# Five early expert tiles regrouped as a pair, a single and a pair

## The chip, the cores and the metric

The kernel runs on one core of one Trainium2 chip. The metric is device microseconds of one execution. The kernel before takes 584.12 us, the median of three runs (583.96 to 584.71). Arithmetic is in float32 wherever a result depends on it.

## The reference

Block-sparse attention is followed by a mixture of eight experts, of which each row takes one:

```
scores = scale * q @ k^T, masked to: near blocks, first and last block, 3 sampled blocks
x = softmax(scores) @ v                          # 4 x 8 heads x 768 x 64 -> 3072 rows of 512
logits = normed(x) @ normed(expert_emb)^T / tau  # 8 experts
e = argmax(logits); gate = softmax(logits)[e]
out[row] = gate * (relu(x[row] @ w1[e]) @ w2[e]) # w1: 512 x 1024, w2: 1024 x 512
```

With the inputs of the reference, expert 0 takes 813 of the 1536 rows of the first two sequences.

## The kernel before

**Attention.** 24 chunks of 128 rows go through steps `s` of a loop that writes out the order of all engines by hand (`attention_fast`). Each step has two places, `planned(0)` and `planned(1)`, where small work is inserted: the routing of finished chunks (`route`), the ranks of rows within their expert (`rank`), and, once the first two sequences are routed, the sixteen stages of `dispatch_early`, one at a time. `after_step` (L1573) says which stage goes to which step. The stages at the first half of step 18 and its second half, and at the first half of step 19, are the ones around the lines L968 to L1082.

**Expert tiles.** Rows are collected by expert into tiles of 128. A first tile set, the `NE` = 5 early tiles, needs only the first two sequences; the late tiles (2 mixed, 7 pairs, 4 singles) need all rows. Units run in the order S S S S S (early), then S P P M P S P M P P S P S. A single (`expert_tile`, L1304) does the first product as 32 matmuls of 128 columns (L1314), a relu, and the second product as 8 matmuls of 512 columns (L1341). A late pair (`pair_tile`, L1418) takes two tiles of one expert as one 2 x 2 block problem and does each product as seven block products in place of eight: sums of weight blocks on VectorE (`weight_sums`, L1361), sums of row blocks on GpSimd (`sum_rows`), and sums of relu blocks on VectorE (`ssum`). Each float32 matmul stands in the trace as two records.

**What moves data.** `fetch_rows` (L1227) gathers rows by indirect DMAs that GpSimd issues: one DMA for each of the first two tiles, four for each later one. `prepare` turns them: TensorE transposes (L1290) for the first two, VectorE transposes (L1295) for the others. Weights come through SyncE, in three buffers. Results go out by an indirect DMA from GpSimd (L1353, L1528).

**The order.** After attention each engine's order is made by a planner from the order of the program text, estimated costs, and explicit edges (`issue_after`: queue what follows behind a given instruction on its engine). The last chunk's logits and routing sit in the second product of the first tile; the last ranks and the first, long part of `dispatch_late` come from the second tile; its last VectorE instruction is `k.lanes_made` (L1008); the slots of late rows follow at the end of the third tile (L1019), the quarter addresses (L1044, L1051) in the fourth, and the first late gathers come right behind them.

Of the kernel before, what the change touches and what calls it, by code (L numbers as in the profile page):

```python
# [20 lines left out]
P = 128  # L21
# [10 lines left out]
G = 128  # L32
EARLY = 2
NE = (EARLY * S - E * (G - 1) + G - 1) // G
MIX = 2
# [3 lines left out]
NU = N // G - NE  # L39
# [21 lines left out]
NL = most_places(N - NE * G)  # L61
# [14 lines left out]
UNITS, ORDER = in_order("SPPMPSPMPPSPS")  # L76
UNIT_OF = {i: u for u, unit in enumerate(UNITS) for i in unit}
# [789 lines left out]
def route(k, b):  # L867
# [30 lines left out]
    picked = nc.vector.tensor_tensor(out=oh, in0=pick, in1=wide(m), op=ALU.is_equal).ins  # L898
    yield
# [57 lines left out]


def tile_experts(k, end, tiles, name):

    nc, p = k.nc, k.dp
    past = p.tile([P, tiles, E], F32, name="past")
    nc.vector.tensor_tensor(out=past, in0=k.tile_no[:, 0:tiles].unsqueeze(2).broadcast_to([P, tiles, E]),
                            in1=end.unsqueeze(1).broadcast_to([P, tiles, E]), op=ALU.is_ge)
    ex = p.tile([P, tiles], F32, name="ex")
    nc.vector.reduce_sum(out=ex, in_=past, axis=AX.X)
    yield
    nc.vector.tensor_scalar(out=ex, in0=ex, scalar1=float(E - 1), scalar2=None, op0=ALU.min)  # L968
    expert = k.const.tile([P, tiles], I32, name=name)
    nc.vector.tensor_copy(out=expert, in_=ex)  # L970
    return expert
# [83 lines left out]
def dispatch_early(k):  # L1055
# [6 lines left out]
    full = p.tile([P, E], F32, name="full")  # L1062
    nc.vector.reduce_sum(out=full, in_=more, axis=AX.X)
    yield
    end = yield from add_up(k, full)
    nc.vector.tensor_scalar(out=end, in0=end, scalar1=float(NE), scalar2=None, op0=ALU.min)
    expert = yield from tile_experts(k, end, NE, "expert_e")
    k.experts = [expert]
    k.taken = k.const.tile([P, E], F32, name="taken")
    base = p.tile([P, E], F32, name="base")  # L1070
    nc.vector.memset(base[:, 0:1], 0.0)
    nc.vector.tensor_scalar(out=base[:, 1:E], in0=end[:, 0:E - 1], scalar1=float(G), scalar2=None, op0=ALU.mult)
    nc.vector.scalar_tensor_tensor(out=k.taken, in0=end, scalar=float(G), in1=base, op0=ALU.mult, op1=ALU.subtract)
    yield
    pos = of_expert(k, base, nt, "pos")
    yield
    late = p.tile([P, nt], F32, name="late")
    taken = of_expert(k, k.taken, nt, "taken_t")
# [121 lines left out]
def parts(i):  # L1200

    if i < NE:
        return [i]
# [823 lines left out]
```

## Time and profile before

| | |
|---|---|
| median of three runs | 584.12 us |
| the profiled execution | 586.81 us |
| its span | 584.9 us |
| TensorE busy | 560.5 us |
| VectorE busy | 329.6 us |
| GpSimd busy | 292.5 us |
| ScalarE busy | 189.8 us |
| granted TensorE clock, mean | 0.993 |

The span goes from the first to the last recorded instruction; the profiled execution's own time is 1.9 us longer. A row of the timeline has its start, its length, the engine, the line, the operation with output and inputs, and in brackets the idle time of the engine just before it with what ended that. A merged row (x16) covers records that follow each other. A row of a table by stretches has, for each engine, busy time and records, then the granted clock, the share of the DMA engines and GB/s.

### The profile page before, as it was taken

How to read it: one execution, taken by the hardware profiler on the slowest of the kernel's cores; microseconds unless marked ns; L12 is line 12 of the kernel's file. 1: busy time of each engine (PE TensorE's matmuls, PEld its weight loads, DVE VectorE, ACT ScalarE, POOL GpSimd, SP SyncE). 2: the span in 40 equal slices, each digit the busy share in tenths (PEclk: the TensorE clock that was granted, in tenths of full speed). 3: DMA queues.
4: the chain of work that ended last, by engine and by line, in shares of the span. 5: the costliest groups of instructions: out<-in, count | busy, mean ns of one | idle time of the engine just before them, and what ended most of it. 6: DMA issues, size and time to landing. Idle time of an engine off the chain costs nothing.

```text
span 584.9 us, 19051 instructions
## 1 busy us (share of the span) xinstructions
PE 560.5 (96%) x7790; PEld 469.1 (80%) x7790; DVE 329.6 (56%) x821; ACT 189.8 (32%) x367; POOL 292.5 (50%) x510
## 2 busy tenths in 40 slices
PE   8999999899999999999999999999999999999995
PEld 5889898798899888877776789739978568987994
DVE  4462687368779972339615576366563296636610
ACT  3545666375655554200000123103112113220310
POOL 2729646346766331442255848276355485836010
PEclk9999999899999999999999999999999999999998
DMA  8979789999998861799999986589987589754000
GB/s 213 244 162 220 170 188 188 195 210 208 205 213 194 204 208 41 269 401 369 399 400 400 393 319 205 184 315 351 391 311 258 193 309 394 273 188 173 10 33 24
DMA packets 167528, 140.72 MB, mean 241 GB/s; under 512 B 135227, under 2 KB 137407, under 8 KB 165128
## 3 DMA queue, kind: packets, MB, share of 16 engines
q1 hardware_dynamic: 161272, 126.25, 70.9%
q0 software_dynamic: 5104, 12.90, 6.1%
q8 instruction: 63, 1.03, 0.7%
q10 hardware_dynamic: 1056, 0.26, 0.2%
q14 instruction: 33, 0.27, 0.1%
HBM read 126.76 MB, written 12.90 MB: 239 GB/s over the span
## 4 chain that ended last, share of the span: by engine, by line
PE 48%; issue 12%; DVE 12%; DMA 11%; POOL 8%; SPq 5%; ACT 2%; POOLq 0%; DVEq 0%; ACTq 0%
PE hp L1314 7%; PE av L701 7%; PE hp L1440 6%; PE yp L1341 5%; POOL xg L1227 5%; DMA out_dram<-y,slot_l 5%; SPq L531 4%; PE yp L1489 4%; PE dps L645 3%; DMA vg<-in_v_dram 3%; DMA xg<-x_dram,quarter 3%; PE xg_ps L1489 2%; PE ac L620 2%; PE bps L676 1%; PE ac L623 1%
## 5 line engine op out<-in xcount | busy, mean ns | idle before, releaser
L1227 POOL DMA_INDIRECT xg<-x_dram,quarter x92 | 100.5, 1092 | 30.4 <-issue 24.4
L1314 PEld LDWEIGHTS hp<-xgt,w 128*128 128x128 f32 x576 | 65.6, 192 | 2.5 <-issue 1.2
L1314 PE MATMUL hp<-xgt,w 128*128 128x128 f32 x576 | 66.4, 276 | 0.8 <-DVE own L1298 0.8
L1341 PE MATMUL yp<-w,h 128*128 128x512 f32 x128 | 57.5, 596 | 1.3 <-issue 1.2
L600 POOL COPY kg<-kt 128x128 f32 x176 | 43.2, 296 | 28.8 <-ACT kt L560 21.0
L543 POOL COPY vg<-vt 32x1040 f32<-32x1040 f32 (+1 forms) x45 | 42.8, 951 | 18.5 <-issue 8.1
L1528 POOL DMA_INDIRECT out_dram<-y,slot_l x14 | 14.2, 1011 | 67.1 <-DVE y L1496 58.6
L645 PEld LDWEIGHTS dps<-qt,kg 128*64 128x64 f32 x1408 | 46.7, 138 | 0.8 <-POOL kg L600 0.6
L645 PE MATMUL dps<-qt,kg 128*64 128x64 f32 x1408 | 46.0, 222 | 0.2 <-POOL kg L600 0.2
L1341 PEld LDWEIGHTS yp<-w,h 128*128 128x128 f32 x128 | 23.3, 190 | 27.7 <-issue 26.6
L620 PE MATMUL ac<-qt,kt 128*64 128x128 f32 x352 | 43.0, 274 | 1.2 <-DVE half L1659 0.5
L623 PE MATMUL ac<-qt,kt 128*64 128x256 f32 (+1 forms) x192 | 42.5, 364 | 0.1
L582 DVE COPY qt<-yp 64x512 f32<-64x512 f32 x48 | 32.9, 685 | 12.1 <-PE yp L577 11.7
L620 PEld LDWEIGHTS ac<-qt,kt 128*64 128x64 f32 x352 | 37.8, 137 | 2.1 <-ACT lg L822 0.9
L650 ACT ACTIVATE pd<-dps,bias 128x256 f32<-128x256 f32 x88 | 34.7, 474 | 10.5 <-PE dps L645 10.4
L587 DVE TENSOR_REDUCE kg<-kt 128x128 f32 (+2 forms) x136 | 33.6, 317 | 3.0 <-ACT kt L560 1.2
L701 PE MATMUL av<-vg,pd 128*32 128x65 f32 x1408 | 29.5, 222 | 5.9 <-DMA vg<-in_v_dram 4.9
L701 PEld LDWEIGHTS av<-vg,pd 128*32 128x32 f32 x1408 | 23.0, 109 | 12.1 <-DMA vg<-in_v_dram 7.0
L771 ACT ACTIVATE pac<-x 128x512 f32<-128x512 f32 x24 | 15.1, 631 | 43.8 <-DVE x L766 42.4
L1440 PEld LDWEIGHTS hp<-xgt,w 128*128 128x128 f32 x224 | 26.5, 192 | 3.2 <-issue 3.1
L701 PEld LDWEIGHTS av<-st,pac 128*64 128x64 f32 x704 | 23.3, 141 | 5.8 <-issue 4.7
L1489 PE MATMUL yp<-tsum,ssum 128*128 128x256 f32 x112 | 27.0, 384 | 0.8 <-DVE y L1496 0.5
(320 smaller groups left out, 1120.9 us busy)
## 6 DMA issues: line engine op xcount, KB each, us to landing
w<-in_moe_w_dram SPq DMA_DIRECT2D x38, 2048.0 KB
vg<-in_v_dram SPq DMA_DIRECT2D x132, 128.0 KB
kraw<-in_k_dram SPq DMA_DIRECT2D x32, 192.0 KB
x_dram<-x SPq DMA_DIRECT2D x10, 516.0 KB
qraw<-in_q_dram SPq DMA_DIRECT2D x9, 512.0 KB
w<-in_moe_w_dram SPq DMA_DIRECT2D x8, 512.0 KB
vt<-in_v_dram SPq DMA_DIRECT2D x10, 256.0 KB
vt<-in_v_dram SPq DMA_DIRECT2D x5, 512.0 KB
```

The costliest lines, as they stand in the source:

```text
L543: k.nc.gpsimd.tensor_copy(out=k.vg_ring[s % 2][lanes_of(NRAND, g), g, which(i)], in_=k.vt[m][rows, which(i)])
L600: copy(out=t[:, :, g, lanes_of(s, g)], in_=kt[:, :, bass.ds(shift, BLK)])
L620: nc.tensor.matmul(out[0:D, j, half], lhsT=kt[:, j, at:at + D], rhs=qt[:, j, :, D * half:D * (half + 1)], start=True, stop=True)
L623: nc.tensor.matmul(out[D:P, j, half:2].rearrange("p f h t -> p h f t"), lhsT=kt[:, j, S:S + D], rhs=qt[:, j, :, D * half:P].rearrange("p h ...
L645: nc.tensor.matmul(out[D * r:D * (r + 1), NG * j + g], lhsT=kg[:, j, g, D * r:D * (r + 1)], rhs=qt[:, j, :, cols], start=True, stop=True)
L650: nc.scalar.activation(e[:, :, g].rearrange("p j h t -> p j (h t)"), out.rearrange("p (j g) h t -> p j g (h t)", g=NG)[:, :, g], ACT.Exp, ...
L701: k.nc.tensor.matmul(av[lanes, h // NPAIR, h % NPAIR * P:h % NPAIR * P + D + 1], lhsT=lhsT, rhs=rhs, start=first[0], stop=last, skip_group ...
L1227: k.nc.gpsimd.indirect_dma_start(out=x[:, g], out_offset=None, in_=quarters, in_offset=bass.IndirectOffsetOnAxis(ap=k.quarters[late][:, g, ...
L1314: k.inner = nc.tensor.matmul(hp[:, f, :], lhsT=w1[:, d, (f0 + f) * P:(f0 + f + 1) * P], rhs=xt[:, d, :], start=(d == 0), stop=(d == ND - 1 ...
L1341: k.summed = nc.tensor.matmul(yp, lhsT=h[:, f, :], rhs=w2[:, f, :], start=(f == 0), stop=(f == NF - 1)).ins
L1440: nc.tensor.matmul(ps[:, f], lhsT=left[:, d, f * P:(f + 1) * P], rhs=right[:, d], start=start and f == 0 and d == 0, stop=d == ND // 2 - 1 ...
L1489: nc.tensor.matmul(out, lhsT=left[:, c], rhs=right[:, c], start=start and c == 0, stop=c == half - 1, skip_group_check=True)
```

## The change

The five early tiles are no longer five singles. They are three units: tiles 0 and 1 as a pair, tile 2 as a single, tiles 3 and 4 as a pair (`UNITS`). An early pair does a plain first product, 32 matmuls of 256 columns (`plain_first`), and the second one by seven block products, with weight sums of `w2` and relu sums on VectorE but none for `w1`. It issues the product of the first block first and releases the next transposes behind `z4`.

`dispatch_early` now finds up to two pairs of full tiles and one more full tile per expert; it has four per-row look-ups (`of_expert`) where it had two, and eight small GpSimd instructions. The three weight sets of the early units replace five. Late places `NL` go from 24 to 28, of which 20 run as before.

Rows of tiles 0 and 1 are fetched together in the second half of step 22 into a buffer of the ring of `x` (before: tile 0 in the first half of step 22, tile 1 after attention), and turned in the second half of step 23 and the first half of step 24 (before: tile 1's turn inside the first tile).

The last logits and the last routing move from the second product of the first tile into its first product (after blocks 1, 2 and 4 of 8); the last ranks and the long part of `dispatch_late` follow the first block of its second product. The slots come after block 4 of the second early pair, the quarter addresses and the gathers of the first two late units after its block 6. The transposes of tiles 3 and 4 are no longer queued behind `k.lanes_made`; the weight sums of the second early pair are.

```diff
-    units, order = [[i] for i in range(NE)], []
+    units, order = [[0, 1], [2], [3, 4]], []
+EARLY_AT = [0, 1, ONLY, 2, 3]
...
 def dispatch_early(k):
-    full = p.tile([P, E], F32, name="full")
-    nc.vector.reduce_sum(out=full, in_=more, axis=AX.X)
+    upto = p.tile([P, 2, E], F32, name="pairs_full")
+    nc.vector.reduce_sum(out=upto[:, 1], in_=more, axis=AX.X)
+    nc.vector.reduce_sum(out=upto[:, 0], in_=more[:, :, 1::2], axis=AX.X)
...
+    nc.gpsimd.tensor_tensor(out=used, in0=end, in1=start, op=ALU.subtract)
+    nc.gpsimd.tensor_scalar(out=last, in0=used[:, 0], scalar1=2.0 * G, scalar2=None, op0=ALU.mult)
+    nc.gpsimd.tensor_scalar(out=base, in0=start[:, 0], scalar1=2.0 * G, scalar2=None, op0=ALU.mult)
+    nc.gpsimd.tensor_scalar(out=k.taken, in0=used[:, 1], scalar1=float(G), scalar2=None, op0=ALU.mult)
+    nc.gpsimd.tensor_tensor(out=k.taken, in0=k.taken, in1=last, op=ALU.add)
+    nc.gpsimd.tensor_scalar(out=shift, in0=start[:, 1], scalar1=float(G), scalar2=float(ONLY * G), op0=ALU.mult,
+                            op1=ALU.add)
+    nc.gpsimd.tensor_tensor(out=shift, in0=shift, in1=last, op=ALU.subtract)
+    nc.gpsimd.tensor_tensor(out=shift, in0=shift, in1=base, op=ALU.subtract)
     yield
-    pos = of_expert(k, base, nt, "pos")
+    pos, last_t = of_expert(k, base, nt, "pos"), of_expert(k, last, nt, "last_t")
     yield
-    taken = of_expert(k, k.taken, nt, "taken_t")
+    shift_t, taken = of_expert(k, shift, nt, "shift_t"), of_expert(k, k.taken, nt, "taken_t")
     yield
+    nc.vector.tensor_tensor(out=pos, in0=pos, in1=here, op=ALU.add)
+    nc.vector.tensor_tensor(out=last_t, in0=here, in1=last_t, op=ALU.is_ge)
+    nc.vector.tensor_tensor(out=last_t, in0=last_t, in1=shift_t, op=ALU.mult)
+    nc.vector.tensor_tensor(out=pos, in0=pos, in1=last_t, op=ALU.add)
+    nc.vector.tensor_tensor(out=taken, in0=here, in1=taken, op=ALU.is_ge)
+    nc.vector.scalar_tensor_tensor(out=pos, in0=taken, scalar=2.0 * N, in1=pos, op0=ALU.mult, op1=ALU.add)
...
 def expert_tile(k, i):
-        elif i >= WHOLE:
+        else:
             nc.scalar.activation(h[:, half:NF], hp, ACT.Relu)
-            k.relu = k.lanes_made if i == WHOLE else k.made
-        else:
-            k.relu = nc.vector.tensor_scalar(out=h[:, half:NF], in0=hp, scalar1=0.0, scalar2=None, op0=ALU.max).ins
+            k.relu = k.made
...
+def plain_first(k, i, w1, w2, xt, h, after):
+    nc = k.nc
+    banks = pair_banks(k, i)
+    for f in range(NF):
+        ps = banks[f // 2].rearrange("p (f r) t -> p f r t", r=DUO)
+        for d in range(ND):
+            k.inner = nc.tensor.matmul(ps[:, f % 2], lhsT=w1[:, d, f * P:(f + 1) * P], rhs=xt[:, d], start=d == 0,
+                                       stop=d == ND - 1).ins
+        if f % 2:
+            nc.scalar.activation(h[:, f - 1:f + 1], ps, ACT.Relu)
+        after.get(f, lambda: None)()
+    return second_weights(k, w2, None if k.exact else k.lanes_made if i else k.picked)
...
+    made = subtract(k, z4, a(0, 1), z2), subtract(k, z3, a(0, 0), a(1, 0))
+    k.relu = made[0 if early else 1]
...
+    begin = [(q2, a(0, 1), b21), (q1, a(0, 0), b11)]
+    for n, what in enumerate(begin[::-1] if early else begin):
+        second(*what, n == 0)
...
-        plan += [(s + 9, 0, partial(fetch_rows, n, 0))]
+        plan += [(s + 9, 1, partial(fetch_rows, n, i)) for i in range(WHOLE)]
-        plan += [(s + 10, 1, partial(prepare, n, 0))]
+        plan += [(s + 10 + i, 1 - i, partial(prepare, n, i)) for i in range(WHOLE)]
...
+        fetch_rows(n, WHOLE)
+        expert_tiles(n, {1: halfway, 2: lambda: part_logits(n, NS - 1), 4: last_route, NF: last_rank},
+                     {NF // 2: late_slots, NF - 2: lambda: next(n.late), NF + 3: partial(count_good, n)})
```

## Rows read from the trace of the kernel before

**Rows 1.** The page, first part: busy time, share of the span, instructions.
```profile
PE 560.5 (96%) x7790; PEld 469.1 (80%) x7790; DVE 329.6 (56%) x821; ACT 189.8 (32%) x367; POOL 292.5 (50%) x510
```

**Rows 2.** By stretch: one of attention, the early stage, the late stage.
```profile
180.00:190.00 10.00, 9.63 (x274) 8.79 (x270) 9.48 (x35) 4.92 (x14) 6.73 (x20) 1.00 0.85 210
...
237.10:314.15 77.05, 74.72 (x459) 53.72 (x457) 36.37 (x146) 6.85 (x16) 32.51 (x42) 1.00 1.02 385
...
314.15:577.60 263.45, 261.24 (x1657) 215.78 (x1655) 144.32 (x194) 53.70 (x96) 137.73 (x123) 1.00 0.69 250
```

**Rows 3.** Timeline of TensorE, the five early tiles and the first late units.
```profile
244.53 0.60 PE L1290 MATMUL xg_ps<-ident,xg 128*128 128x128 f32 x4
244.97 4.82 PE L1341 MATMUL yp<-w,h 128*128 128x512 f32 x10
249.63 0.60 PE L781 MATMUL xg_ps<-ident,x 128*128 128x128 f32 x4
...
283.17 0.25 PE L1019 MATMUL slot_ps<-val,lanes 128*128 128x48 bf16 x3 [0.22 <-DVE lanes L1008]
284.16 3.84 PE L1314 MATMUL hp<-xgt,w 128*128 128x128 f32 x32 [0.75 <-DVE own L1298]
...
291.60 7.03 PE L1341 MATMUL yp<-w,h 128*128 128x512 f32 x16
298.46 7.31 PE L1314 MATMUL hp<-xgt,w 128*128 128x128 f32 x64
305.61 3.60 PE L1341 MATMUL yp<-w,h 128*128 128x512 f32 x8
310.39 1.13 PE L1341 MATMUL yp<-w,h 128*128 128x512 f32 x2 [1.19 <-issue]
...
328.17 1.95 PE L1440 MATMUL hp<-xgt,w 128*128 128x128 f32 x16
...
551.41 3.62 PE L1489 MATMUL yp<-w,h 128*128 128x256 f32 x16
554.86 1.89 PE L1489 MATMUL xg_ps<-tsum,h 128*128 128x256 f32 x8
```

**Rows 4.** Timeline of attention, steps 17 to 19: VectorE, and a waiting TensorE.
```profile
178.02 0.98 DVE L943 COPY end<-end 128x4 f32<-128x4 f32 x1
...
187.57 0.25 DVE L978 TENSOR_TENSOR at_e<-oh,base 128x96 f32<-128x96 bf16 x1
...
190.76 0.64 PE L800 MATMUL xg_ps<-xt,en 128*32 128x256 f32 x8 [0.85 <-DVE xt L784]
...
192.84 0.17 DVE L1081 TENSOR_TENSOR pos<-pos,rank 128x12 f32<-128x12 f32 x1
```

**Rows 5.** Timeline of the last step of attention: TensorE and the copy behind it.
```profile
230.25 0.67 PE L701 MATMUL av<-vg,pd 128*32 128x65 f32 x32
230.35 0.69 DVE L784 COPY xt<-xg_ps 128x512 f32<-128x512 f32 x1 [0.89 <-PE xg_ps L781]
```

**Rows 6.** Timeline of GpSimd around the second half of step 22.
```profile
219.00 0.47 POOL L902 TENSOR_TENSOR seen<-seen,oh 128x8 bf16<-128x8 bf16 x2 [5.58 <-DVE oh L898]
```

**Rows 7.** Timeline of VectorE: the late dispatch, weight sums, relu sums.
```profile
263.17 0.16 DVE L1099 TENSOR_TENSOR cnt<-count,taken 128x8 f32<-128x8 f32 x1
...
279.75 3.36 DVE L1008 TENSOR_TENSOR lanes<-lane,low 128x384 bf16<-128x384 f32 x7
...
332.42 1.23 DVE L1361 TENSOR_TENSOR tsum<-w 128x1024 f32<-128x1024 f32 x1
...
341.56 0.69 DVE L1444 TENSOR_TENSOR ssum<-h 128x512 f32<-128x512 f32 x1 [2.92 <-ACT h L1469]
```

**Rows 8.** Timeline of the late gathers: quarter addresses, GpSimd's issues, first row sum.
```profile
288.72 0.27 DVE L1051 TENSOR_SCALAR quarter<-quarter_got,group 128x96 int32<-128x96 f32 x1
...
291.06 0.99 POOL L1227 DMA_INDIRECT xg<-x_dram,quarter  x1 [0.31 <-issue]
...
327.52 0.74 POOL L1412 TENSOR_TENSOR xsum<-xgt 128x256 f32<-128x256 f32 x1
```

More of the change, by code (lines that the diff above doesn't have):

```diff
@@ L1067, in dispatch_early @@
-    expert = yield from tile_experts(k, end, NE, "expert_e")
+    for step in (1, 2, 4):
+        nxt = p.tile([P, 2, E], F32, name=f"early{step}")
+        nc.vector.tensor_copy(out=nxt[:, :, 0:step], in_=upto[:, :, 0:step])
+        nc.vector.tensor_tensor(out=nxt[:, :, step:E], in0=upto[:, :, step:E], in1=upto[:, :, 0:E - step], op=ALU.add)
+        upto = nxt
+        yield
+    edge = p.tile([P, 2, E + 1], F32, name="early_ends")
+    end, start = edge[:, :, 1:], edge[:, :, 0:E]
+    nc.vector.memset(edge[:, :, 0:1], 0.0)
@@ L1327, in expert_tile @@
                 first_sums(k, i)
-        if after and f0 - NF in after:
-            after[f0 - NF]()
     yp = ring(k, "yp", i, 1, k.eps, [P, DM])
@@ L1415, in sum_rows, with add, pair_banks, block @@
     subtract(k, s[3], a(0, 1), s[1], k.nc.gpsimd)
[L1418 to L1426 removed]
+def add(k, out, one, other, engine=None):
+    return (engine or k.nc.vector).tensor_tensor(out=out, in0=one, in1=other, op=ALU.add).ins
+def pair_banks(k, i):
+    return [ring(k, f"hp{f0}", i + j, 2, k.hps, [P, NF // 2, P]) for j in range(2) for f0 in (0, NF // 2)]
+def block(h, r, c):
+    half = NF // 2
+    return h[:, half * c:half * (c + 1), r]
+def second_weights(k, w2, behind):
+    with k.tc.issue_after(behind) if behind is not None else ExitStack():
+        return weight_sums(k, w2, [ring(k, f"tsum{j}", 0, 1, k.wp2, [P, NF // 2, DM // 2]) for j in range(3)])
+def seven_first(k, i, w1, w2, xt, h):
+    nc, half, a = k.nc, NF // 2, partial(block, h)
     (b11, _), (b21, b22) = four_blocks(w1)
@@ L1485, in pair_tile @@
     y0, y1 = (ring(k, "y", i + j, 2, k.wp2, [P, DM]) for j in range(2))
+    made = iter(range(NF, NF + 7))
     def second(out, left, right, start=False):
         for c in range(half):
-            nc.tensor.matmul(out, lhsT=left[:, c], rhs=right[:, c], start=start and c == 0, stop=c == half - 1,
-                             skip_group_check=True)
+            k.inner = nc.tensor.matmul(out, lhsT=left[:, c], rhs=right[:, c], start=start and c == 0,
+                                       stop=c == half - 1, skip_group_check=True).ins
+        after.get(next(made), lambda: None)()
     def scaled(out, ps, gate):
@@ L1847, in expert_tiles @@
         elif second_half:
-            pair_tile(n, i)
+            pair_tile(n, i, hooks.get(i, {}))
         else:
-            expert_tile(n, i, {0: after, 1: second and {NF // 2 - NF: second}, NE - 2: {-NF: first_late},
-                               NE - 1: spread and {NF // 2: partial(count_good, n)}}.get(i))
-        next(between, None)
+            expert_tile(n, i)
 def last_tiles(n):
```

189 lines of the change are left out of this document (89 added, 100 removed).

## The prediction

> **What bounds the kernel now.** I read the page's busy times first: TensorE is busy for 560.5 of 584.9 us [rows 1], so time can only be saved where TensorE has less to do or waits. The table by stretches then splits the span: the five early tiles take 77.05 us with TensorE busy for 74.72, the late units up to the last product 263.45 with 261.24 busy [rows 2]. The granted clock is 1.00 in all of these, the 2.4 GHz level, so no term below is a clock term. Last I read the timeline of TensorE in the early stage, tile by tile, to separate products from insertions and waits [rows 3]. The late units are not touched except in when their rows arrive; I leave their length as it is and price only their start.
>
> The profiled execution took 586.81 us, 1.9 more than its span and 2.7 more than the median of 584.12. All terms below are differences within its span; I subtract them from the median.
>
> **Products (A).** A single's first product starts at 298.46 and its second at 305.61: 7.15 us for 32 matmuls of 128 columns. A second product runs from 291.60 to 298.46: 6.86 us [rows 3]. Two singles are 28.02. In an early pair the second product is seven blocks of four matmuls with 256 columns. In the late pair two such blocks take from 551.41 to 554.86, 3.45 [rows 3], so seven take 12.08, against 13.72. The plain first product is 32 matmuls of 256 columns. The trace has none of that input, but the second product's blocks have the same shape: eight matmuls in 3.45, so 13.80, against 14.30. I take that, as the operation is the same; the upper end is 14.30, if a wider matmul gains nothing. A pair is 25.88, 2.14 less; two pairs 4.28 less (3.28 at the other end). Fewer weight loads are hidden under the matmuls already.
>
> **Waits that go (B).** 77.05 us less five times 14.01 leaves 7.0 us of insertions and waits. Three waits belong to the old form. In the first tile, ten records of the second product should take 4.29 (16 take 6.86) and the next row starts 4.66 later, at 249.63: 0.37, behind a relu that VectorE made late. At the third tile's end TensorE waits 0.22 for the lanes and 0.75 for the fourth tile's rows, which were queued on VectorE behind the lanes: 0.97. In the fifth there is a wait of 1.19 in the middle of the second product [rows 3]. The change gives all early relus to ScalarE, takes the edge to the lanes away from the transposes, and makes the fifth tile half of a pair. I count all three as gone, 2.53. The first two have a named cause that leaves; the third has "issue" as its releaser and may come back, so the low end is 1.34; the high end is 3.7, all of what is left of the 7.0 when the insertions that stay (about 2.9) and 0.44 of transposes are taken out. What the slots of late rows wait for next is VectorE (below).
>
> **Transposes of tile 1 (C).** They take 0.44 in the stage (244.53 to 244.97 [rows 3]) and move into attention's last step, right behind the turn of a chunk into the same PSUM tile. VectorE copies that turn out until 231.04, and TensorE's next work starts at 230.25 [rows 5]. In an order written by hand the new transposes wait there: 0.80 us, and the weighing queued behind them with them. So C is +0.80 net. It is nothing at the low end, should the later wait for ScalarE's exponentials absorb it. The fetch itself is one more GpSimd issue, where GpSimd is idle for 5.58 us before 219.00 [rows 6].
>
> **Early dispatch on VectorE (D).** Two more look-ups of two instructions at 0.25 each are 1.0 us at the second half of step 18, three more small instructions at 0.17 are 0.5 at step 19 [rows 4]; what the earlier stages gain and lose is within 0.4. VectorE is busy for 9.48 of 10 us from 180 to 190 [rows 2], and right after step 18 TensorE already waits 0.85 for a copy by VectorE [rows 4]. There is no cover there: I take the whole 1.5 as lost. It is 0 if VectorE's small idle times take it. Eight small GpSimd instructions come before these look-ups and can make VectorE wait: a copy of four columns took 0.98 on VectorE, others of that size 0.17 [rows 4], while GpSimd copied. Twice that excess, 1.6, is the upper addition, so 3.1 at the high end. The Trainium skill ("SBUF — State Buffer", section "SBUF: two separate sides") says that VectorE and GpSimd hold one port pair by an exclusive lock for a whole instruction, and the 0.98 against 0.17 agrees; by it the eight new instructions would speak for the high end of D, and the sum would be about 1.6 us worse.
>
> **Last routing, ranks, late dispatch on VectorE.** Let zero be the start of the first pair. Its first product lasts 13.80 with 1.45 of insertions (transposes, logits) and its second 12.08 with 0.2 for the ranks, so the single starts at 27.5 and the second pair at 41.5. The last logits come after five of eight blocks, near 10.1, and the last choice of experts near 11.9. VectorE then has: four weight sums at 1.23, 4.9; four relu sums at 0.69, 2.7; the transposes of tile 2, 1.4 with their gate; ranks, 0.7; the late dispatch from 263.17 to 283.11, 19.2 without the result copy inside it, and some 0.6 for NL at 28; three gated results, 1.4 [rows 7]. That ends at 42.9, if the transposes of tiles 3 and 4 (2.8) are elsewhere. The weight sums are done at 16.8 and their first user starts at 15.3 + 3.7 = 19.0: no wait. The lanes are needed after five blocks of the second pair, at 50: no wait. I take 0 for all of this; the danger is in the fourth rival.
>
> **Late rows (E).** Now the quarter addresses are ready at 289.0 [rows 8], 25 us before the first late single at 314.15 [rows 2]. After the change they are ready some 14.6 us into the second pair (seven blocks at 1.73, slots 1.1, addresses and their wait 1.4), which lasts about 27.2: 12.6 us before that single. GpSimd issues a gather every 1.3 [rows 8]. Twelve gathers for the two late units end at 3.7 us after the single's start; the first four land in time. One result, four gathers, one result, four gathers follow, as now eight gathers stand ahead of the first row sum (327.52, against a pair that starts at 328.17 [rows 3, 8]). The sum comes at 17.5 after the single's start; the pair's second block product needs it at 14.0 + 1.8 = 15.8. So TensorE waits 1.7. The ends are 0 (the planner puts the sums ahead of four gathers) and 3.0 (GpSimd's instructions are stretched by 5%, as 23 of them last 30 us).
>
> **Sum.** -4.28 - 2.53 + 0.80 + 1.5 + 1.7 = -2.8. 584.1 - 2.8 = 581.3. Two weight sets of 4 MB fewer are loaded while the DMA engines are at 1.02 of their share [rows 2]; no wait of TensorE in the stage names a weight, so I give nothing for it.
>
> **Rivals.** *1. The additions hide.* D and E are 0: -6.0, 578.1. For it: VectorE is idle by 5% around step 18, and the order of GpSimd is free to put row sums first. Against: the wait of 0.85 names VectorE.
> *2. The saving is half of it.* A is 3.28 and the 1.19 stays: -2.8 + 1.0 + 1.2 = -0.6, 583.5. For it: that wait has no named cause. Against: the same shape is seen at its speed.
> *3. It does not do what it says*: too few full tiles for two pairs, so tiles are computed for nothing and more run at the end, 14 us each. The inputs give expert 0 six full tiles among the early rows, which are three pairs; I leave it at 0.02, near 612.
> *4. The other side: the second pair's rows queue behind the late dispatch.* The planner puts the transposes of tiles 3 and 4 behind the lanes, though no edge asks for it. Then they end at 42.9 + 2.8 = 45.7 and the second pair, due at 41.5, waits 4.2: -2.8 + 4.2 = +1.4, 585.5. For it: the dispatch stands earlier in the text, and the VectorE work between fits only by 1.4 too little. Against: a result copy was let in in the middle of that chain. It decides from where more than about two thirds of the late dispatch stands ahead of both transposes.
>
> **Numbers.** Forecast 0.44 (own range 579.5 to 582.9), rival 1 0.22, rival 2 0.14, rival 3 0.02, rival 4 0.18. A measurement of this kernel can tell 0.2%, 1.17 us, from no change. Forecast and rival 1 are faster, 0.66; rival 2 is the same, and of rival 4 a small part is: 0.16; the rest, 0.18, is slower. The range goes from 577.2 (below rival 1 by the spread of B) to 585.7 (with half of rival 4).
>
> **What would show it.** A: block products of 1.73 and a first product of 13.8 in the early pairs. C and D: the first expert matmul at 239.8 in place of 237.10; much earlier says D is hidden. B: the first late single 69.8 us after that, at 309.6. E: the first late pair at 323.7, and a wait for `xsum` in it. Rival 4 would show as a wait of the second early pair for `own` or `xgt` by VectorE. The prediction is wrong if the early stage, first expert matmul to first late single, is longer than 73 us.

## The result and the profile after

The changed kernel took 592.47 us (median of 4 runs) against 584.41 for the kernel before on the same chip (4 runs): 1.0133, interval 1.0102 to 1.0164. That is 8.1 us slower, where 2.8 less was forecast. The profiled execution took 591.05 (span 589.3), against 586.81.

First the page's busy times, then the table by stretch (the columns of [rows 2]): the whole early stage, and the two blocks of a second product in it that matter below.

```profile
PE 557.4 (95%) x7710; PEld 476.9 (81%) x7710; DVE 347.9 (59%) x846; ACT 194.1 (33%) x377; POOL 304.1 (52%) x520
...
241.27:320.03 78.76, 72.74 (x376) 60.41 (x374) 49.96 (x161) 11.25 (x25) 34.94 (x42) 0.96 0.85 312
...
261.70:265.08 3.38, 3.38 (x10) 2.67 (x9) 2.46 (x9) 0.00 (x0) 2.77 (x3) 0.53 1.02 417
...
313.07:316.57 3.50, 3.50 (x8) 2.85 (x9) 0.24 (x3) 0.00 (x0) 2.58 (x4) 0.51 0.23 59
```

TensorE is busy 3.1 us less than in [rows 1], and the span is 4.4 longer: TensorE has less to do, and more than that was lost in waits. The early stage, forecast at 69.8 us, took 78.76. TensorE's timeline shows where (start, duration, line, operation, and in brackets the idle time before it with what ended it):

```profile
241.27 2.86 PE L1505 MATMUL hp<-xgt,w 128*128 128x256 f32 x12
...
257.03 1.89 PE L1544 MATMUL yp<-w,h 128*128 128x256 f32 x8
261.60 0.19 PE L932 MATMUL rk<-seen,ones_b 128*128 128x56 bf16 x1 [2.68 <-POOL seen L905]
261.70 3.59 PE L1544 MATMUL yp<-w,h 128*128 128x256 f32 x8
...
313.07 3.66 PE L1544 MATMUL yp<-tsum,ssum 128*128 128x256 f32 x8 [3.35 <-DVE y L1552]
316.57 1.89 PE L1544 MATMUL xg_ps<-w,ssum 128*128 128x256 f32 x8
...
320.03 7.31 PE L1336 MATMUL hp<-xgt,w 128*128 128x128 f32 x64
...
334.04 1.95 PE L1469 MATMUL hp<-xgt,w 128*128 128x128 f32 x16
339.06 2.05 PE L1469 MATMUL hp<-xsum,x 128*128 128x128 f32 x16 [1.29 <-POOL xsum L1377]
```

The first expert matmul starts at 241.27 (239.8 was forecast, 237.10 in [rows 2]) and the first late pair at 334.04 (323.7; 328.17 in [rows 3]). The two blocks from 316.57 to 320.03 take 1.73 each, as forecast. But there are two waits that the kernel before does not have in this stage. The matmul that ranks the last routed tokens waits 2.68 for GpSimd's count `seen`; the second pair's fifth block waits 3.35 for VectorE's gated result `y`, whose PSUM bank it needs. Behind each, the next block takes 3.38 and 3.50, twice its time, and the granted clock there is 0.53 and 0.51, the 1.2 GHz level.

What made the two releasers late stands in the queues of their own engines. GpSimd, then two stretches of VectorE:

```profile
254.88 1.14 POOL L909 TENSOR_TENSOR gate<-ex_l 128x2 f32<-128x2 f32 x1
...
256.80 1.81 POOL L1251 DMA_INDIRECT xg<-x_dram,quarter  x1 [0.48 <-issue]
258.64 0.32 POOL L905 TENSOR_TENSOR seen<-seen,oh 128x8 bf16<-128x8 bf16 x1
259.11 1.94 POOL L1251 DMA_INDIRECT xg<-x_dram,quarter  x1 [0.15 <-issue]
261.08 0.47 POOL L905 TENSOR_TENSOR seen<-seen,oh 128x8 bf16<-128x8 bf16 x1
...
254.74 1.23 DVE L1377 TENSOR_TENSOR tsum<-w 128x1024 f32<-128x1024 f32 x1
...
258.94 1.22 DVE L1377 TENSOR_TENSOR tsum<-w,tsum 128x1024 f32<-128x1024 f32 x1
...
311.29 1.08 DVE L1317 STREAM_TRANSPOSE xgt<-xg 128x512 f32<-128x512 f32 x1 [5.66 <-DMA xg<-x_dram,quarter]
...
312.54 0.48 DVE L1552 SCALAR_TENSOR_TENSOR y<-yp,gate,u 128x256 f32<-128x256 f32 x1
```

The two additions to `seen`, 0.3 and 0.5 us long, stand between the gathers of the second pair's rows, near 1.9 us each. The gated result, 0.48 long, stands behind the transposes of the first late single, and these wait 5.66 for that single's gathered rows. In both cases a short instruction that TensorE needs now is queued behind one that serves a later tile.

For `seen` the order alone is not all of it. GpSimd in the kernel before has the same order:

```profile
256.33 0.19 POOL L906 TENSOR_TENSOR gate<-ex_l 128x2 f32<-128x2 f32 x1
...
257.32 1.11 POOL L1227 DMA_INDIRECT xg<-x_dram,quarter  x1 [0.51 <-issue]
258.47 0.21 POOL L902 TENSOR_TENSOR seen<-seen,oh 128x8 bf16<-128x8 bf16 x1
258.84 1.02 POOL L1227 DMA_INDIRECT xg<-x_dram,quarter  x1 [0.16 <-issue]
259.90 0.21 POOL L902 TENSOR_TENSOR seen<-seen,oh 128x8 bf16<-128x8 bf16 x1
```

There the second addition ends at 260.11, and the ranks are asked for at 261.00, 23.9 us after the first expert matmul. In the changed kernel they are asked for 17.5 us after it. And GpSimd takes 6.67 us from the start of `gate` to the end of the second addition, where the kernel before takes 3.78: the instructions that run beside VectorE's sums for the pair's second product, back to back from 254.74 on but for one short pause, got longer. With the lengths of the kernel before, the second addition would end 2.9 us earlier and the wait of 2.68 would be gone (an estimate from these rows). What makes GpSimd slower there was not tested.

### The profile page after: what moved, and what is told of

Read it like the earlier page. It is cut to its first block, busy times and chain, and to the rows that moved or that the text cites. A ratio compares the mean times of both kernels' runs of the same rounds, so it can differ in the third digit from the quotient of the medians.

```text
span 589.3 us, 18923 instructions
## 1 busy us (share of the span) xinstructions
PE 557.4 (95%) x7710; PEld 476.9 (81%) x7710; DVE 347.9 (59%) x846; ACT 194.1 (33%) x377; POOL 304.1 (52%) x520
## 4 chain that ended last, share of the span: by engine, by line
PE 35%; issue 21%; POOL 14%; DMA 14%; DVE 8%; SPq 4%; ACT 2%; POOLq 1%; DVEq 0%; ACTq 0%
POOL xg L1251 8%; PE hp L1469 6%; PE av L703 5%; PE dps L647 4%; DMA xg<-x_dram,quarter 4%; PE yp L1544 4%; DMA out_dram<-y,slot_e 3%; DMA out_dram<-y,slot_l 3%; SPq L533 3%; DMA vg<-in_v_dram 3%; PE hp L1336 2%; PE xg_ps L1544 2%; PE ac L622 2%; PE ac L625 2%; POOL xsum L1377 2%
## 5 line engine op out<-in xcount | busy, mean ns | idle before, releaser
L1251 POOL DMA_INDIRECT xg<-x_dram,quarter x92 | 103.0, 1120 | 33.4 <-issue 25.4
L1544 PE MATMUL yp<-tsum,ssum 128*128 128x256 f32 x144 | 36.0, 395 | 3.6 <-DVE y L1552 3.3
L1336 PEld LDWEIGHTS hp<-xgt,w 128*128 128x128 f32 x320 | 36.5, 192 | 0.3
L1336 PE MATMUL hp<-xgt,w 128*128 128x128 f32 x320 | 36.5, 275 | 0.0
L1544 PEld LDWEIGHTS yp<-tsum,ssum 128*128 128x128 f32 x144 | 28.2, 198 | 8.5 <-DVE y L1552 4.5
L1552 DVE SCALAR_TENSOR_TENSOR y<-xg_ps,gate,u 128x256 f32<-128x256 f32 x16 | 7.7, 482 | 45.5 <-PE xg_ps L1544 33.3
L1544 PE MATMUL yp<-w,h 128*128 128x256 f32 x144 | 34.4, 393 | 0.0
L1544 PE MATMUL xg_ps<-w,ssum 128*128 128x256 f32 x144 | 34.0, 379 | 0.0
L1549 ACT ACTIVATE u<-yp,gate 128x256 f32<-128x256 f32 x24 | 11.4, 473 | 62.1 <-PE yp L1544 62.1
```

The lines of the kernel that those rows point to most:

```text
L1251: k.nc.gpsimd.indirect_dma_start(out=x[:, g], out_offset=None, in_=quarters, in_offset=bass.IndirectOffsetOnAxis(ap=k.quarters[late][:, g, ...
L1336: k.inner = nc.tensor.matmul(hp[:, f, :], lhsT=w1[:, d, (f0 + f) * P:(f0 + f + 1) * P], rhs=xt[:, d, :], start=(d == 0), stop=(d == ND - 1 ...
L1544: k.inner = nc.tensor.matmul(out, lhsT=left[:, c], rhs=right[:, c], start=start and c == 0, stop=c == half - 1, skip_group_check=True).ins
```

## The experiments

Two theories stood at the start. The main one: those two orders cost the time, each with its half-clock block. The rival: the losses lie elsewhere, in attention (terms C and D) or in stretches in which TensorE waits for nothing that the trace names; then taking the waits away gains little. Kernels that ran together on one chip share the runs of the kernel before on it, and ratios are to these. "Stage" is from the first expert matmul to the first late single.

**The kernel after again (e0_again).** No edit.

> The changed kernel once more, unaltered, for a second profile and more times. My theory is that the loss stands in fixed places of the early stage: the rank matmul of the first pair waits again some 2.8 us for GpSimd's seen, the fifth block of the second pair waits again some 3.6 us for VectorE's y, and each is followed by a block of about 3.4 us at half the granted clock; the stage from the first expert matmul to the first late single is again 78 to 79 us. Rival: the two waits are accidents of one execution (where DMAs happened to land); then one of them is under 1 us here and the stage under 76.

597.42 against 593.66: 1.0081 [1.0046, 1.0116]. Both waits again, 2.67 and 3.37; only the second was followed by a block at half clock. Stage 77.58.

**The count ahead of the gathers (e1_seen).**

```
+ k.counted = nc.gpsimd.tensor_tensor(out=k.seen[:, t + 1, :], ...).ins
+ if WHOLE < i < NE and not k.exact:      # in the fetch of rows
+     order.enter_context(k.tc.issue_after(k.counted))
```

> The gathers of the fourth and fifth tile are not issued before GpSimd's last addition of the seen counts. My theory: the first pair's rank matmul no longer waits (2.84 us) and the block after it runs at full granted clock, 1.73 in place of 3.38 (1.65): 4.5 us less than the changed kernel. Rival 1, the slow block has another cause than the wait before it: only 2.8 less. Rival 2, the later gathers make the second pair's rows late: the saving comes back as a wait of the second pair for own or xgt, 0 in all.

1.0007 [0.9969, 1.0045], stage 74.87; the median, 593.69, is 3.7 under that of e0_again. The wait for `y` stays (3.50). GpSimd now does both additions in one go ahead of the gather, and the rank matmul has no wait:

```profile
260.49 1.34 POOL L905 TENSOR_TENSOR seen<-seen,oh 128x8 bf16<-128x8 bf16 x2
261.99 2.01 POOL L1254 DMA_INDIRECT xg<-x_dram,quarter  x1 [0.15 <-issue]
...
262.84 0.19 PE L933 MATMUL rk<-seen,ones_b 128*128 128x56 bf16 x1
262.89 1.97 PE L1547 MATMUL yp<-w,h 128*128 128x256 f32 x8
```

**The gated result ahead of the late single's transposes (e2_y0).**

```
- prepare_next(k, i + 1)
+ if not early or i == 0:
+     prepare_next(k, i + 1)
  ... after the result of the first half is gated:
+ if early and i > 0:
+     k.relu = k.made
+     prepare_next(k, i + 1)
```

> In the second early pair the transposes of the late single, which wait for its gathered rows, are traced behind the y gate of the pair's first half. My theory: the gate no longer stands behind them on VectorE, block 5 of the pair does not wait 3.6 us, and the block after it runs at full granted clock (3.50 becomes 1.73): 5.4 us less than the changed kernel. Rival: the late single's transposes then come so late that its first product waits for them; of the 5.4 some 1.5 to 3 stay. Second rival: the gate is late because the late dispatch chain on VectorE is long, not because of the transposes; then less than 1 us is saved.

The wait for `y` is gone and the stage is 73.59, yet the ratio is 1.0112 [1.0069, 1.0155]: the first late single took 24.05 (322.61 to 346.66) instead of 14.0, with gaps in its first product as shown for the next run.

**Both edits (e3_both).**

> Both orders at once. My theory: the two waits are independent, so 4.5 + 5.4 = 9.9 us less than the changed kernel, at 582 to 583, about 2 us under the kernel before. Rival, the loss is the pair form itself or attention's longer chain: under 3 us is saved. Third case, the waits share a cause (VectorE's chain starts later without the first wait's cover): between 5 and 8.

1.0064 [1.0028, 1.0101]. Stage 69.53, the forecast's 69.8. But again the first late single took 23.07. TensorE's timeline, then ScalarE's, then the stretches:

```profile
312.28 1.89 PE L1548 MATMUL yp<-tsum,ssum 128*128 128x256 f32 x8
314.01 3.17 PE L1339 MATMUL hp<-xgt,w 128*128 128x128 f32 x27
318.97 0.27 PE L1339 MATMUL hp<-xgt,w 128*128 128x128 f32 x1 [1.13 <-issue]
...
320.43 0.47 ACT L1553 ACTIVATE u<-yp,gate 128x256 f32<-128x256 f32 x1 [8.80 <-remote]
...
314.01:321.00 6.99, 4.46 (x33) 3.76 (x31) 0.54 (x2) 0.47 (x1) 5.15 (x7) 1.00 0.73 187
321.00:328.00 7.00, 4.47 (x17) 3.85 (x18) 6.12 (x10) 0.00 (x0) 5.17 (x5) 0.52 0.70 253
```

The gaps have "issue" as releaser. ScalarE reads the block that the trace ends near 314.0 only at 320.43, after idling 8.80; in e3_again (below), which has no such gaps, it reads the same block 0.1 after its recorded end. TensorE really was late, from a point before the gaps that the modelled ends show. From 314 to 321 the granted clock is 1.00 all the same; from 321 to 328 it is 0.52. So a further loss had come in the place of the wait; whether it is there without the edits was the next question.

**The kernel before, seen again (b0_before).** No edit.

> The kernel before, unaltered, for a second profile taken beside the changed ones. Its ratio should be 1.000. My theory of the attention part: its first expert matmul comes 2.5 to 3 us earlier than in a changed kernel of the same chip (1.4 for the earlier dispatch, 1.05 for the tile's transposes). My theory of slow phases (TensorE runs at less than half its speed at a granted clock of 1.00, with no wait that names a releaser): this kernel has them too, at the end of the early stage and in the third late pair; its early stage is again 77 us with a wait without a named releaser in the fifth tile. Rival: that wait of 1.19 was an accident and the stage is 76 or less.

1.0023 [0.9989, 1.0057]. The same thing in the kernel before, in the fifth tile's second product: 309.50 to 322.72 is 13.2, where [rows 3] have 6.86 for such a product. Stage 81.74, longer than that of any unaltered changed kernel. The first expert matmul stands at 240.98, and at 245.43 to 248.13 in the three changed kernels of this chip, 4.5 to 7.2 later where 2.5 to 3 was expected.

```profile
309.50 3.60 PE L1341 MATMUL yp<-w,h 128*128 128x512 f32 x8
315.83 2.08 PE L1341 MATMUL yp<-w,h 128*128 128x512 f32 x2 [2.74 <-issue]
...
322.72 1.50 PE L1314 MATMUL hp<-xgt,w 128*128 128x128 f32 x12
```

**TensorE kept busy in both waits (e4_busy).** Extra matmuls with the identity in front of the rank matmul (24) and of the second pair's fifth block (28).

```
+ nc.tensor.matmul(ps[:, 0], lhsT=k.ident, rhs=k.ident, start=True, stop=True)   # x24, x28
```

> The changed kernel, with matmuls of the identity whose result is not used placed in both waits of TensorE (24 before the rank matmul, 28 before the fifth block of the second pair, some 2.7 and 3.1 us); nothing else is moved. Theory 1, TensorE's speed depends on how long it has worked without a rest: the half-clock blocks after the waits are gone (up to 3.4 less), but TensorE now falls into a slow phase at the end of the second pair or in the late single, as when the waits themselves were taken away, and the late single takes over 20 us from its first matmul to the late pair's in place of 14: 3 to 9 us slower than the changed kernel. Theory 2, the slow late single came from the moved order on VectorE: no slow phase here, and 0 to 3.4 us less than the changed kernel.

1.026 [1.0202, 1.0318]. The gaps fell into the extra matmuls themselves, whose one input never changes:

```profile
317.35 3.60 PE L1454 MATMUL hp<-ident 128*128 128x128 f32 x30
322.84 0.27 PE L1454 MATMUL hp<-ident 128*128 128x128 f32 x1 [1.15 <-issue]
```

So these gaps are no wait for rows, weights or a bank. The extra matmuls were priced at half of what they take: the 24 before the rank matmul last 5.36 us (265.61 to 270.97), where they were to fill 2.7, so the edit costs time by itself. The block behind them took 1.97 at a granted clock of 1.00; but it took 1.97 in e0_again too, behind the wait, so whether keeping TensorE busy saves the clock could not be read here. The late single took 14.0.

**The count, the bank and the row sums (e7_all).** To e1_seen come: the transposes of tile 1 in attention's last step go into another PSUM bank (term C), and the gathers of the first late pair are issued behind GpSimd's row sums of the unit before (term E).

```
+ if i == 1 and not k.exact:
+     ps = ring(k, "yp", 0, 1, k.eps, [P, DM]).rearrange(...)
...
- ... if UNIT_OF[NE] <= UNIT_OF[i] < len(UNITS) - 2
+ ... if UNIT_OF[NE] <  UNIT_OF[i] < len(UNITS) - 2
  ... after the row sums:
+ for t in UNITS[UNIT_OF[i] + 2] if i == NE else ():
+     fetch_rows(k, t)
```

> The changed kernel with three orders altered: gathers of the fourth and fifth tile behind the last seen addition (-3.7 as measured alone), tile 1's transposes through another PSUM bank (-0.8: no wait of 0.79 for the copy xt by VectorE), and in the first late single the gathers of the unit after next behind the row sums (-1.3 to -1.5: no wait for xsum in the first late pair). My theory: the sum of the three, 5.8 less than the changed kernel, which puts it 1 us under the kernel before on this chip. Rival: what is saved before the late stage comes back as a wait there or as a slow phase of TensorE; then 3.7 or less, the same as the kernel before.

1.0105 [1.0054, 1.0156]. The wait for `y` stays (3.64) and TensorE was slow later, from 344 to 362, in the first late pair; there it waits 2.39 and 1.96 for ScalarE's `h`, and ScalarE in its turn idles 3.72 with "issue" as releaser.

**e3_both with a rest (e8_pause).** A chain of eight ScalarE copies, which the second pair's products wait for.

```
+ for j in range(8):
+     nc.scalar.copy(out=rest, in_=rest if j else yp[:, 0:192])
+ for ps in banks:      # second pair's first product
+     nc.scalar.copy(out=ps[:, 0, 0:1], in_=k.rest[:, 0:1])
```

> Both waits removed as in e3_both, and a rest for TensorE put in between the single and the second pair: a chain of 12 copies on ScalarE, some 4 us, before the pair's first matmul. Theory 1 (TensorE slows down for want of a rest): the wait is there, some 3.5 to 4.5 us with a half-clock block behind it, and the late single that took 23 us takes 14 to 16 again; 0 to 5 us less than e3_both. Theory 2 (the slow late single comes from the moved order on VectorE): the late single takes 23 us again and the kernel is 3.5 to 6 slower than e3_both.

1.0182 [1.0131, 1.0234]. The rest cost 3.30 and a half-clock block; gaps came all the same between 316 and 330, though fewer: the first late single took 16.1 instead of 23.1, not far from the 14 to 16 of theory 1; but the ratio, on another chip, is above that of e3_both, not under it.

**The kernel after on another chip (a1_after).** No edit.

> The changed kernel, unaltered, beside the three below on one chip. My theory: 0.6 to 1.4% slower than the kernel before; first expert matmul 4 to 6 us later than the kernel before had it on such a chip (240.98 there), the waits for seen (2.7) and for y (3.6) in place. Rival: the later start of the early stage was scatter of the attention part; then it starts within 1.5 us of 241.

595.84 against 592.64: 1.0067 [1.004, 1.0094]. The first expert matmul comes at 248.08, 7.1 us behind the 240.98 of b0_before, so the rival's 1.5 is far off, and more is lost ahead of the stage than the 4 to 6 expected. Both waits are there (2.69 and 3.24).

**The count alone, again (v1_two).** The edit of e1_seen.

> The gathers behind the last seen addition alone, once more on this chip: of the orders tried it is the one that paid. My theory: 3.7 less than the changed kernel here too, and within 0.3% of the kernel before. Rival, slow phases of TensorE take it back on a chip that has more of them: under 1.5 less than the changed kernel.

1.0007 [0.9977, 1.0038], as the first time. By the ratios that is 3.6 us under a1_after, by the medians (594.14 and 595.84) 1.7, so the expected 3.7 is not settled.

**Look-ups spread (v2_spread).** The count and the bank, and the four look-ups in attention spread over two more half steps:

```
+ yield        # between the look-ups
- ... n.dispatching) for i in range(16)]
+ ... n.dispatching) for i in range(18)]
```

> As v1_two, with tile 1's transposes through another PSUM bank (-0.8), and the four look-ups of the early dispatch spread over two half steps more, so that two of them stand before and two behind the copy xt that TensorE waits for after step 18. My theory of D: the wait for that copy falls from 1.9 to 0.9 and ScalarE's exponentials past it stand 0.5 to 1 later than in the kernel before in place of 2.1: with the bank, 1.8 to 2.4 less than v1_two, so faster than the kernel before by about 2 us. Rival: VectorE has no idle time in the later half step either and the lanes come later; then only the 0.8 of the bank is seen, or the first pair waits for its rows, whose gather is issued a half step later.

1.0065 [1.0038, 1.0092]. The delay at step 18 was gone (-0.05 against the kernels with the old form), and 3.8 came back in attention's last step, so in attention the work only moved. The time says little about it: the first late single took 19.5 instead of 14.0, with gaps like those of e3_both.

**The look-ups alone, in the kernel before (d1_lookups).** The instructions that the change adds to the early dispatch (two look-ups, eight small GpSimd and three small VectorE ones), their results unused.

```
+ of_expert(k, extra[0], nt, "extra_a")
+ extra_b = of_expert(k, extra[3], nt, "extra_b")
```

> The kernel before with the instructions added to the early dispatch and nothing else of the change: two more look-ups and three small operations on VectorE and eight small operations on GpSimd, whose results are not used. My D: the exponentials of the attention steps behind it come 1.5 later than in the kernel before (0 to 3.1), and 1.5 us of its time, 0.25%, follow. Rival 1: it is 2 to 3.3, as between the profiles of the two kernels (GpSimd's operations stretch VectorE's). Rival 2: nothing, the shift seen there comes from where the rows and the transposes were moved.

1.0026 [1.0, 1.0052]. ScalarE's exponentials stand at the same place in every kernel. Between the same two groups around step 18, first in b0_before, then d1_lookups, then the kernel after (a2_after):

```profile
191.89 0.85 ACT L650 ACTIVATE pd<-dps,bias 128x256 f32<-128x256 f32 x2
198.88 1.57 ACT L650 ACTIVATE pd<-dps,bias 128x256 f32<-128x256 f32 x4
```

```profile
190.45 0.84 ACT L650 ACTIVATE pd<-dps,bias 128x256 f32<-128x256 f32 x2
199.89 1.56 ACT L650 ACTIVATE pd<-dps,bias 128x256 f32<-128x256 f32 x4
```

```profile
193.56 0.84 ACT L652 ACTIVATE pd<-dps,bias 128x256 f32<-128x256 f32 x2
202.74 1.56 ACT L652 ACTIVATE pd<-dps,bias 128x256 f32<-128x256 f32 x4
```

6.99, 9.44 and 9.18: the added instructions alone cost 2.4, the change 2.2. Of this 0.46 comes back on the way to the next group (7.83 us in b0_before, 7.37 in the other two), so 2.0 and 1.7 are left. That is D. Of the fifteen profiles with the change's look-ups in their place, fourteen have 8.4 to 10.2 for the 9.18; a1_after has 6.75, with 2.8 more in the step ahead.

**Both orders on a chip whose traces show no such gaps (e3_again).** The edits of e3_both.

> Both waits removed, unaltered from e3_both, to stand on one chip beside the kernel with a rest. Both theories: the late single again takes over 18 us from its first matmul to the late pair's in place of 14, with gaps that name no releaser; 0.3 to 1.2% slower than the kernel before.

588.95 against 586.25: 1.0048 [1.0019, 1.0078]. Stage 69.52, first late single 14.02, then waits of 3.29 and 0.31 for `xsum` in the first late pair.

**The rest there (e8_again).** The edits of e8_pause.

> The same with the rest of some 3.3 us (and a half-clock block behind it, 3.1 lost) between the single and the second pair. Theory 1, TensorE's lost time depends on how long it has worked without a rest: the stage from the first expert matmul to the late pair is no longer than 1 us above e3_again's, as the slow phase is shorter by nearly what the rest costs. Theory 2, it does not depend on it: 5 to 6.4 longer than e3_again's.

1.0131 [1.0091, 1.017]: 592.42, 3.5 more than e3_again, and 3.5 more from the first expert matmul to the late pair (87.08 against 83.54), which is neither theory's figure. The rest was a wait of 3.28, and this time no half-clock block stood behind it (8.90, where e8_pause has 11.73). Where there are no gaps to shorten, the rest is a plain loss.

**The kernel before with a rest (b2_rest).** A chain of 20 copies of 16 columns ahead of the fifth tile.

```
+ for j in range(20):
+     nc.scalar.copy(out=rest, in_=rest if j else yp[:, 0:16])
```

> The kernel before with a rest for TensorE of some 4 us (22 small copies on ScalarE) ahead of its fifth tile. Theory 1: its wait without a releaser in the fifth tile (1.2 to 2.7) goes, and the stage from the first expert matmul to the first late single is at most 3 us longer than the kernel before's (77 to 82). Theory 2: the wait stays, and the stage is longer by the rest and a half-clock block behind it, 5.5 to 7.

1.0121 [1.008, 1.0163]. The rest is a wait of 4.82, and the product behind it takes 9.45 (7.31 in [rows 3]); the 1.19 without a named releaser is not there. Stage 82.60. The unaltered kernel before was not profiled on this chip, and no other trace of the chip has such gaps in this place, so the run does not show that the rest took the wait away.

**The count and the row sums (v3_sums).**

> As v1_two, with the gathers of the unit after next traced behind the row sums in the first late single, which takes away the first late pair's wait of 1.3 for xsum. Theory 1: TensorE falls into a slow phase late in that pair, as in e7_all (17 us there for what takes 7), and nothing or less than nothing is saved: 0 to 10 us more than v1_two had over the kernel before. Theory 2: 1.3 less than v1_two, so 1 us under the kernel before.

1.007 [1.0038, 1.0102]: 589.1. The waits for `seen` and `xsum` are gone, the one for `y` stays (3.41, and 3.52 for the block behind it). Stage 74.62. No v1_two stands beside it on this chip, so the time does not tell the two theories apart.

**All four orders (v4_four), beside the kernel after (a2_after).** Count, gated result, bank and row sums, each edit as above.

> All four orders at once: gathers behind seen, the y gate ahead of the late single's transposes, tile 1's transposes through another bank, the late gathers behind the row sums. My theory: the stage from the first expert matmul to the first late single is 69 to 70 us, as predicted for the change, no wait for xsum follows, and tile 1's transposes wait no longer; what stays of the loss is in attention (2.2 for the look-ups, 0.6 to 1.2 at its start). Where TensorE has no slow phase this is 4.4 less than e3_again, which was 2.7 over the kernel before: 1 to 2 under it. Where TensorE has slow phases, as in e2_y0 and e3_both, one of 9 to 11 us comes in the late single: 3 to 9 over the kernel before.

> The changed kernel, unaltered, beside it: 0.7 to 1.4% slower than the kernel before, with its three waits (2.7 for seen, 3.3 for y, 1.3 for xsum) whether or not TensorE has slow phases on this chip. If the four orders are worth what their waits cost, v4_four is 7 to 10 less than this.

Before 585.83; v4_four 586.34, 1.0016 [0.9994, 1.0037]; the kernel after 594.61, 1.016 [1.0132, 1.0189]. So the four orders are worth 8.3 us. TensorE's timeline of v4_four, then of a2_after:

```profile
242.76 2.86 PE L1512 MATMUL hp<-xgt,w 128*128 128x256 f32 x12
260.24 0.19 PE L933 MATMUL rk<-seen,ones_b 128*128 128x56 bf16 x1
307.02 1.97 PE L1552 MATMUL yp<-tsum,ssum 128*128 128x256 f32 x8
312.28 7.31 PE L1341 MATMUL hp<-xgt,w 128*128 128x128 f32 x64
326.29 1.95 PE L1476 MATMUL hp<-xgt,w 128*128 128x128 f32 x16
348.84 3.52 PE L1552 MATMUL yp<-tsum,ssum 128*128 128x256 f32 x8 [2.97 <-DVE y L1560]
```

```profile
243.91 2.86 PE L1505 MATMUL hp<-xgt,w 128*128 128x256 f32 x12
264.23 0.19 PE L932 MATMUL rk<-seen,ones_b 128*128 128x56 bf16 x1 [2.68 <-POOL seen L905]
315.81 3.67 PE L1544 MATMUL yp<-tsum,ssum 128*128 128x256 f32 x8 [3.44 <-DVE y L1552]
322.76 7.31 PE L1336 MATMUL hp<-xgt,w 128*128 128x128 f32 x64
```

The stage is 69.52 in the one and 78.85 in the other: 9.3 us for the two orders. In v4_four a new wait of the same kind came, 2.97 for `y` in the first late pair with a half-clock block behind it, some 4.6 in all (2.97 and 3.52 less 1.89). None of these versions beats the kernel before.

## Why the prediction was wrong

The step that failed is "Last routing, ranks, late dispatch on VectorE", priced at 0. It summed VectorE's work and asked whether rows and lanes come in time. They did: the second pair starts its first product without a wait, so rival 4 did not happen. But two other users hung on the same queues and were not asked about. The ranks were taken as a cost of 0.2 on TensorE, not as a reader of GpSimd's `seen`; and the "three gated results, 1.4" were counted as length on VectorE, not as what frees the bank for the fifth block. Putting the two orders right takes both waits away (e3_again, v4_four), so the orders are what the loss hangs on. That GpSimd would need 6.67 us for what took 3.78 was not in the working either; with the earlier need it turns an order that cost nothing before into a wait. Price: 9.3 us of stage (78.85 against 69.52). In the first profile the two waits are 2.68 and 3.35, and the half-clock blocks behind them add 1.65 and 1.77 (3.38 and 3.50 for 1.73).

**A, -4.28: right to about half a microsecond.** With the two orders put right the stage is 69.52 in e3_again and v4_four where the forecast said 69.8. The second pair of e3_again has 12.17 for the seven blocks and, without what is inserted, 13.98 for the first product, where 12.08 and 13.80 were taken: A is about -3.7.

**B, -2.53: right in the stage, by luck as to the third wait.** The two named waits are gone. The third, "issue", stands in three of the four profiles of kernels with the old form (1.19, 2.74, 1.18) and in none of the four of the unaltered changed kernel. But it is a small case of the gaps in b0_before, e3_both and e4_busy, and these come in changed kernels too, so it was not the old form's alone to lose. "May come back" was the right caution.

**C, +0.80: right.** With the 0.44 of transposes that moved, the way from the last exponential to the first expert matmul was to grow by 1.24. It is 19.0 to 20.4 us in the four profiles of kernels with the old form, 19.7 on average, and 19.8 to 21.7, on average 20.9, in the thirteen of the new form without the other bank: 1.2 more, with a scatter as large as that. The turn's own wait is there as argued, 0.8, in the list of waits by line of the kernel after:

```profile
PE xg_ps L1312 <- DVE xt L786: 0.8, 1, 0.8
```

**D, +1.5: a little low, inside its range.** 2.2 at the place (9.18 less 6.99) and 1.7 after the next group, 2.4 and 2.0 in d1_lookups: the added instructions cost more than their own lengths. d1_lookups adds the GpSimd instructions and the look-ups together, so it does not tell which of them does it; the rule of the Trainium skill ("SBUF — State Buffer", section "SBUF: two separate sides") that spoke for the high end of 3.1 is neither shown nor refuted by it.

**E, +1.7: right.** A wait of 1.29 for `xsum` in the first late pair (1.15 and 1.29 in a1_after), and none in v3_sums and v4_four, where the row sums stand ahead of the gathers as its low end and rival 1 had it.

**Not foreseen:** the first exponential comes 0.4 to 0.8 us later in the changed kernels (2.1 and 2.3 in two profiles; 17.39 in b0_before, 18.00 in a2_after), behind instructions that are the same in both. Its cause was not found. In the later traces attention drifts further: the first expert matmul stands at 237.10 to 240.98 in the four profiles of kernels with the old form and at 241.27 to 249.02 in the sixteen of the new one, on average 6.1 later, where C, D and this make 3.5 to 3.8. These are single executions that scatter by 4 to 8 us; no run shows where the rest comes from.

Together, in the two profiled executions, where the span grew by 4.4 and the sum said -2.8: the first expert matmul came 1.4 later than forecast (241.27 for 239.84), the stage was 9.0 longer (78.76 for 69.8), and from the first late single to the end it took 269.27 against 270.75 before, 3.2 less than with the forecast's +1.7. That makes 7.2. The last part is scatter: this stretch takes 267.95 to 275.4 in the four profiles of kernels with the old form. The medians miss by 10.9, because the profiled execution of the kernel before lay 2.4 above its median of 584.41 and that of the changed kernel 1.4 below its own.

**Open.** What causes the gaps without a releaser. They were seen on the three chips of the runs from e0_again to d1_lookups, in both kernels, and not in the early stage or the first late units of any trace of the two chips after; on the chips that show them the change costs 0.7 to 0.8% instead of 1.3 to 1.6%, which fits a kernel before that loses there too, but no run separates that. On one chip they do not stand in every kernel: e2_y0 and e3_both have them, e0_again and e1_seen, where a half-clock block stands in the second pair, do not. v2_spread, where no such block stands behind the wait, has them. But e3_again and v4_four have neither such a block there nor gaps, so this alone does not decide it. Whether a rest shortens them is not settled either: e8_pause had fewer, and nothing else.

## What to carry to other kernels

When a step gets shorter, ask of every engine's queue what stands ahead of each short instruction whose result TensorE needs next, even one that costs next to nothing: sums of busy time do not show it. Ask it again when the need moves earlier: the order that made `seen` late stood in the kernel before and cost nothing there. Price a wait of some 3 us at one and a half times to nearly twice its length (4.33 for 2.68, 5.12 for 3.35, 6.23 for 3.30 in e8_pause), since the block behind it may run at half clock. And check a repair beyond its own stage: with both waits removed, the next stood in the first late pair (3.29 for `xsum` in e3_again, 2.97 for `y` in v4_four).

## What the runs showed of the hardware

A wait of about 3 us was mostly, not always, followed by a stretch at the 1.2 GHz level. Of ten waits for the gated result between 2.97 and 3.64 all but one (v2_spread, 3.41) were followed by a block of 3.4 to 3.8 instead of 1.9; of five for `seen` at 2.67 to 2.69, three (3.4 to 3.6), while in e0_again and a1_after the block took 1.97. Behind 3.29 for `xsum` in e3_again came none. Of two rests in the same place, 3.30 was followed by 11.73 us instead of 8.80 (e8_pause, granted clock 0.50 in the first 3.3 of them), 3.28 by 8.90 (e8_again).

TensorE can run far below its speed with a granted clock of 1.00 and no releaser in the trace (from 317 to 321 in e3_both it is busy for 1.48 of 4.00 us at 1.00), also on matmuls that wait for nothing (e4_busy, 1.15 idle before 322.84). Such a stretch is seen from its readers: ScalarE's idle 8.80 in e3_both, 6 us past the recorded end of the block that it reads.

A gather issued by GpSimd holds its queue: 1.81 and 1.94 us for the two around the additions to `seen` (2.01 in e1_seen), 1.00 to 1.02 for the next four, 0.99 in [rows 8]; an addition of 0.3 us behind it is as late as that.

GpSimd's instructions were longer while VectorE made sums back to back (254.74 to 261.49): `gate` 1.14 us instead of 0.19, two gathers 1.81 and 1.94 instead of 1.11 and 1.02, two additions 0.32 and 0.47 instead of 0.21. The one at 256.10, in the pause between two sums, took 0.21 as before. All four profiles of the unaltered changed kernel show this to 0.02 us. That VectorE's sums are the cause was not tested.
